# Sliding-window attention into a gated MLP: value loads requested nine steps later, and one transpose split by head halves

## The chip, the cores and the metric

The kernel runs on one core of a Trainium2 chip. The metric is the device time of one execution in microseconds (us), here the median of several runs of the same program. A profile of one execution shows what each engine did: PE (matrix multiply) and PEld (its weight loads), DVE (vector), ACT (activation), POOL (GpSimd), and SP, which only issues DMAs in this kernel.

## The reference

Attention with an ALiBi bias and a window of 128 keys over 8 batches of 8 heads, 576 tokens, head size 64; its output, as rows of 512, goes through two matrix products with a gate between them.

```python
scores = scale * np.matmul(q, k.transpose(0, 1, 3, 2))
bias = slopes[:, None, None] * (-np.abs(rel).astype(np.float32))[None, :, :]
mask = (rel >= 0) & (rel < window)
scores = np.where(mask, scores + bias[None], -1000000000.0)
attn = np.exp(scores - max) / sum          # softmax over the keys
x = np.matmul(attn, v)                     # heads side by side: [4608, 512]
h = x @ w_in                               # [4608, 2048]
g = h * (1.0 / (1.0 + np.exp(-beta * h)))
out = g @ w_out                            # [4608, 512], float32
```

## The kernel before, in words

**Tiling.** A batch has five blocks of queries and keys, four of 128 rows and one of 64 (ROWS). `load_qk` (L123) requests q and k of one block on SP's queue (L95, float32 into the staging tiles `fst`, 13 buffers) and returns a cast that POOL does later into `bst` (L129, 8 buffers, bf16). `TD` (L250, L253) transposes a cast block into `qkT` with two DMA transposes, q first, also on SP's queue; `qkT` has two copies, by batch parity. Batches 0 to 2 are transposed on PE instead (`TP`, L229, copied by L234, and `TT`). `load_v` (L134) fetches the values of one block: for batches 3 to 7 (NTE = 3) POOL issues a DMA that casts on its way (L137) straight into `vs`, which has two copies by batch parity; for batches 0 to 2 SP loads them and POOL casts (L142).

`SC` (L262) makes scores: matmuls of keys with queries into PSUM (L290) and the exponential on ACT (L303, or L298 for batches 0 and 1), then a mask on DVE (L307). `PV` (L319) multiplies the weights with the values (L330 and L334; a column of ones gives the sum), four heads at a time (g = 0 or 1), and DVE divides by the sum (L339, L340) into `xn`. `X` (L346) transposes the 512 columns of a finished block of `xn` into `XT`: by four PE transposes (L358) into a PSUM tile of the two-buffer pool `psum_t` and one copy by ACT or DVE (L363), and for batches above 3 by a DMA transpose on SP (L354).

The second part works on groups of 512 tokens: `HS` (L368) makes one 128-wide piece of h (L377: four matmuls, over the four 128-row pieces c of `XT`), with a tanh on ACT (L382) and the gate on DVE (L383). `OS` (L387) sums four matmuls of the output (L393); its sixteenth is scaled by ACT (L408) and stored by POOL (L411).

**Order.** The order of PE's instructions is written out by hand, and from batch 2 on that of SP and POOL too. The start of batch 0 is a straight list (from L589): scores, then for each block the second four heads of PV and the transpose of the block before, and then the first H group. From L651 on, `steps` lists the attention work; `merge` (L493) lays loads, casts and DMA transposes between the steps, each at a due step number counted from `first[b]`, the step at which batch b's scores begin (L507 to L511). A batch takes 21 to 23 steps. `spread` (L434) then interleaves these with the H and output pieces in proportion to costs; the laid-in loads cost zero.

The lines that the change touches:

```python
t0 = first[b] - 26 + 4.3 * sb                          # q and k of block sb requested
jobs.append((t0 + 4.5, lambda c=casts: c.pop()()))     # cast on POOL
jobs.append((t0 + 8.5, lambda b=b, sb=sb: TD(b, sb)))  # transposes on SP
vals(b, sb, first[b] - 16 + 3 * sb)                    # values requested on POOL
```

## Time and profile before

| what | value |
|---|---|
| median of 6 runs | 330.33 us (329.11 to 331.66) |
| the profiled execution's own time | 330.55 us |
| its span, first to last instruction | 328.6 us |
| PE, PEld busy | 314.9, 155.1 us |
| DVE, ACT, POOL busy | 193.6, 213.3, 107.3 us |
| SP's DMA queue (q1), POOL's (q0) | 105744 packets, 31.60 MB; 30224 packets, 15.54 MB |
| values by POOL (L137) | 25 requests, median 5.8 us from issue to landing for the 128-row ones |
| q and k loads by SP (L95, L109) | medians 5.0 and 5.8 us |

A line of the profile names a source line, an engine, what is written and read, and a count. In the timeline the first two numbers are the start and the length in microseconds; a bracket at the end is idle time of the engine before the instruction and what ended it. In the table by stretches a line gives the stretch, its length, busy time and instruction count of PE, PEld, DVE, ACT and POOL, the granted PE clock, the mean busy share of the 16 DMA engines (above 1 where packets of several queues overlap) and GB/s. In the list of waits a line gives who waited for whom, the total, the number of waits and the longest. The chain that ended last is followed backwards from the last instruction, at each step to what released it; "SPq" in it is SP's queue issuing, "DMA" the way from issue to landing.

### The profile page before, as it was taken

Reading aid. Unit: us, or ns where it says so; the run is one execution under the profiler, and the core shown is the slowest. Engines: PE = TensorE matmul, PEld = TensorE weight load, DVE = VectorE, ACT = ScalarE, POOL = GpSimd, SP = SyncE. Lnnn points to the kernel's source line nnn. Section 1 sums busy time; section 2 is a strip of 40 time slices with the busy share of each in tenths; the row PEclk is TensorE's granted clock in tenths of the full one; section 3 lists DMA queues with packets and bytes.
Section 4 is the critical chain, followed back from the end, with each engine's and each line's share of the span. In section 5 each row is a group of like instructions: output and inputs, shape, how many; then the busy total and the mean of one; then the engine's idle time right before and its main releaser. Section 6 shows DMA issues by size and latency. Waiting matters only on the chain.

```text
span 328.6 us, 6187 instructions
## 1 busy us (share of the span) xinstructions
PE 314.9 (96%) x2258; PEld 155.1 (47%) x2300; DVE 193.6 (59%) x421; ACT 213.3 (65%) x413; POOL 107.3 (33%) x173
## 2 busy tenths in 40 slices
PE   8978999999999999999999999999999999999995
PEld 3454445444544555454445444444445444444442
DVE  6657768995436777666666666666665443344400
ACT  5657685887787777777777777777774444454421
POOL 3754584155633545342443243500000000010000
PEclk9999999999999999999999999999999999999999
DMA  7999999999999999999999999934122200001011
GB/s 184 244 181 296 177 273 210 206 205 166 196 219 165 186 187 211 222 154 183 152 208 144 208 171 175 157 74 51 40 66 66 72 32 32 34 32 60 36 66 64
DMA packets 136174, 47.67 MB, mean 145 GB/s; under 512 B 123200, under 2 KB 133712, under 8 KB 136144
## 3 DMA queue, kind: packets, MB, share of 16 engines
q1 hardware_dynamic: 105744, 31.60, 54.1%
q0 software_dynamic: 30224, 15.54, 29.7%
q8 instruction: 18, 0.29, 0.4%
q10 hardware_dynamic: 176, 0.14, 0.1%
q14 instruction: 12, 0.10, 0.1%
HBM read 36.71 MB, written 9.44 MB: 140 GB/s over the span
## 4 chain that ended last, share of the span: by engine, by line
PE 68%; DMA 18%; SPq 8%; POOL 2%; issue 1%; DVE 0%; ACT 0%; POOLq 0%
PE ops L393 33%; PE hps L377 28%; DMA fst<-in_k_dram 8%; DMA fst<-in_v_dram 6%; DMA fst<-in_q_dram 4%; SPq L253 3%; SPq L109 3%; PE sps L290 3%; SPq L95 2%; PE pv L334 2%; PE pv L330 1%; DMA qkT<-bst 1%; POOL vs L142 1%; POOL bst L129 1%; POOL W L193 0%
## 5 line engine op out<-in xcount | busy, mean ns | idle before, releaser
L382 ACT ACTIVATE sig<-hps,beta_h 128x512 bf16<-128x512 f32 x144 | 99.8, 695 | 78.5 <-PE hps L377 61.3
L377 PE MATMUL hps<-XT,W 128*128 128x512 bf16 x554 | 144.2, 379 | 2.0 <-ACT XT L363 0.7
L393 PE MATMUL ops<-W,gT 128*128 128x512 bf16 x560 | 143.7, 379 | 1.4 <-issue 0.3
L383 DVE SCALAR_TENSOR_TENSOR gT<-sig,hps 128x512 bf16<-128x512 bf16 x144 | 98.3, 684 | 63.8 <-ACT sig L382 63.5
L393 PEld LDWEIGHTS <-gT 128*128 128x128 bf16 x576 | 53.5, 98 | 62.7 <-issue 2.1
L377 PEld LDWEIGHTS <-W 128*128 128x128 bf16 x576 | 51.5, 97 | 52.9 <-issue 3.0
L303 ACT ACTIVATE pt<-sps,bias 128x256 bf16<-128x256 f32 (+1 forms) x192 | 72.8, 492 | 2.1 <-PE sps L290 2.1
L129 POOL CAST bst<-fst 128x512 bf16<-128x512 f32 (+1 forms) x50 | 32.3, 648 | 78.9 <-DMA fst<-in_q_dram 45.9
L307 DVE TENSOR_TENSOR pt<-pt,mask 128x1024 bf16<-128x1024 bf16 x48 | 34.6, 720 | 34.7 <-ACT pt L303 34.5
L411 POOL DMA_DIRECT2D out_dram<-osb x32 | 17.9, 560 | 90.3 <-ACT osb L408 90.3
L340 DVE TENSOR_TENSOR xn<-pv,zs 128x256 bf16<-128x256 f32 (+1 forms) x80 | 33.7, 422 | 2.6
L408 ACT ACTIVATE osb<-ops 128x512 f32<-128x512 f32 x35 | 20.9, 597 | 15.2 <-PE ops L393 15.2
L334 PE MATMUL pv<-vs,pt 128*128 128x65 bf16 x320 | 28.7, 193 | 1.0 <-POOL vs L142 0.6
L334 PEld LDWEIGHTS <-pt 128*128 128x128 bf16 x320 | 21.6, 97 | 10.3 <-issue 0.6
L330 PE MATMUL pv<-vs,pt 128*128 128x65 bf16 x256 | 24.1, 193 | 0.3 <-DVE XT L363 0.3
L330 PEld LDWEIGHTS <-pt 128*128 128x128 bf16 x256 | 20.1, 98 | 7.5 <-issue 1.0
L290 PE MATMUL sps<-qkT 64*128 64x256 bf16 (+2 forms) x320 | 21.9, 251 | 1.8 <-DVE qkT L234 0.8
L298 ACT ACTIVATE pt<-sps 128x1024 bf16<-128x1024 f32 x16 | 16.3, 1023 | 8.8 <-PE sps L290 8.3
L137 POOL DMA_DIRECT2D vs<-in_v_dram x25 | 21.3, 853 | 0.6 <-issue 0.5
L290 PEld LDWEIGHTS <-qkT 64*128 64x128 bf16 x320 | 11.2, 94 | 20.1 <-issue 14.0
L339 DVE RECIPROCAL zs<-pv 128x4 f32<-128x4 f32 (+1 forms) x80 | 14.0, 176 | 10.4 <-PE pv L334 10.1
L113 POOL CAST bst<-fst 128x512 bf16<-128x512 f32 x24 | 14.5, 621 | 14.5 <-DMA fst<-in_q_dram 11.4
(49 smaller groups left out, 112.6 us busy)
## 6 DMA issues: line engine op xcount, KB each, us to landing
fst<-in_q_dram SPq DMA_DIRECT2D x32, 256.0 KB, 5.0
fst<-in_k_dram SPq DMA_DIRECT2D x32, 256.0 KB, 5.8
out_dram<-osb POOLq DMA_DIRECT2D x32, 256.0 KB, 3.4
fst<-in_v_dram SPq DMA_DIRECT2D x12, 256.0 KB, 6.5
vs<-in_v_dram POOLq DMA_DIRECT2D x20, 128.0 KB, 5.8
W<-in_moe_w_in_dram POOLq DMA_DIRECT2D x4, 512.0 KB, 7.9
W<-in_moe_w_out_dram POOLq DMA_DIRECT2D x4, 512.0 KB, 14.0
fst<-in_q_dram SPq DMA_DIRECT2D x8, 128.0 KB, 4.1
```

The costliest lines, as they stand in the source:

```text
L129: nc.gpsimd.tensor_copy(out=t[0 : ROWS[sb], i], in_=f)
L137: nc.gpsimd.dma_start(out=to, in_=v[b, :, P * sb : P * sb + ROWS[sb], :].rearrange("h p d -> p h d"))
L290: nc.tensor.matmul(o, lhsT=qk[64 * e : 64 * e + 64, 1, p, P * kb : P * kb + P], rhs=qk[64 * e : 64 * e + 64, 0, p, P * kb : P * kb + nq], ...
L303: nc.scalar.activation(out=pt[:, e, cols], in_=sps[e][:, cols], func=ACTF.Exp, scale=qscale, bias=bias[:, half, h : h + 1],)
L307: nc.vector.tensor_tensor(out=pt[:], in0=pt[:], in1=masks[m][:].rearrange("p (o c) -> p o c", o=1).broadcast_to([P, 2, 512]), op=ALU.mult,)
L330: nc.tensor.matmul(pv[:, hl, 0 : D + 1], lhsT=weights(b, qb - 1, h, 1), rhs=vs[:, qb - 1, h, 0 : D + 1], start=True, stop=False,)
L334: nc.tensor.matmul(pv[:, hl, 0 : D + 1], lhsT=weights(b, qb, h, 0), rhs=vs[:, qb, h, 0 : D + 1], start=qb == 0, stop=True,)
L340: nc.vector.tensor_tensor(out=xn[0:nq, 4 * g : 4 * g + 4, :], in0=pv[0:nq, :, 0:D], in1=zs[0:nq].broadcast_to([nq, 4, D]), op=ALU.mult,)
L377: nc.tensor.matmul(hps[:], lhsT=W1[:, c, bass.ts(j, P)], rhs=XT[:, c, c0 : c0 + TOKG], start=(c == 0), stop=(c == NDM - 1),)
L382: nc.scalar.activation(out=sig[:], in_=hps[:], func=ACTF.Tanh, scale=beta_h[:, j : j + 1])
L383: nc.vector.scalar_tensor_tensor(out=gts[g][:, j, :], in0=sig[:], scalar=1.0, in1=hps[:], op0=ALU.add, op1=ALU.mult)
L393: nc.tensor.matmul(ops_[:], lhsT=gT[:, j, i * P : i * P + P], rhs=W2[:, j, :], start=(j == 0), stop=(j == NFF - 1),)
```

## The change

**Values.** For batches 3 to 7 the request of block sb's values moves from step `first[b] - 16 + 3 * sb` to `first[b] - 7 + 3 * sb`. The due steps of q, k, casts and transposes stay.

**Head halves.** `X` takes an optional half. With half 0 it transposes the first two 128-column pieces (heads 0 to 3) and copies these; with half 1 the other two. Each call takes a PSUM tile of its own from `psum_t`. For block 3 of batch 0, the last block that the first H group reads, half 0 now stands before that block's second PV, and half 1 where the whole transpose stood.

```diff
-    def X(b, qb):
+    def X(b, qb, half=None):
         nq = ROWS[qb]
-        xnv = xns.pop((b, qb))[:].rearrange("p h d -> p (h d)")
+        cs = range(NDM) if half is None else range(2 * half, 2 * half + 2)
+        xnv = (xns[b, qb] if half == 0 else xns.pop((b, qb)))[:].rearrange("p h d -> p (h d)")
...
         xt = psum_t.tile([P, NDM, P], BF16, name="xt", tag="t")
-        for c in range(NDM):
+        for c in cs:
             nc.tensor.transpose(
                 out=xt[:, c, :], in_=xnv[:, c * P : (c + 1) * P], identity=ident[:]
             )
         copy = nc.vector.tensor_copy if b in (1, NTE) or (b, qb) == (0, 2) else nc.scalar.copy
+        c = slice(cs[0], cs[-1] + 1)
         for at, r0, r1 in parts:
-            copy(out=XT[:, :, at : at + r1 - r0], in_=xt[:, :, r0:r1])
+            copy(out=XT[:, c, at : at + r1 - r0], in_=xt[:, c, r0:r1])
...
-                vals(b, sb, first[b] - 16 + 3 * sb)
+                vals(b, sb, first[b] - 7 + 3 * sb)
...
                 if qb:
                     X(0, qb - 1)
-            X(0, NQB - 2)
+                if qb == 2:
+                    X(0, 3, 0)
+            X(0, 3, 1)
```

## The prediction

> **What bounds the kernel now.** I read the page first: busy shares, then the chain that ended last.

> ```profile
> PE 314.9 (96%) x2258; PEld 155.1 (47%) x2300; DVE 193.6 (59%) x421; ACT 213.3 (65%) x413; POOL 107.3 (33%) x173
> ...
> PE 68%; DMA 18%; SPq 8%; POOL 2%; issue 1%; DVE 0%; ACT 0%; POOLq 0%
> ```

> TensorE is busy for 96% of the span, so the most that any reordering can return is its idle time, 328.6 - 314.9 = 13.7 us. Yet a quarter of the chain is DMA and SP's queue. The table by stretches says where:

> ```profile
> 74.00:84.00 10.00, 9.68 (x88) 5.07 (x89) 4.31 (x11) 7.22 (x19) 5.01 (x8) 1.00 1.51 171
> 84.00:99.00 15.00, 13.99 (x118) 7.01 (x118) 7.52 (x17) 11.03 (x27) 8.42 (x13) 1.00 1.29 207
> 99.00:125.00 26.00, 25.79 (x198) 13.21 (x198) 17.51 (x38) 19.39 (x42) 11.16 (x17) 1.00 1.33 176
> 125.00:310.00 185.00, 183.69 (x1203) 88.97 (x1225) 106.23 (x212) 121.47 (x238) 43.48 (x68) 1.00 0.68 112
> ```

> The first two numbers of a line are its length and PE's busy time. From 99 us to 310 us PE idles 1.5 of 211 us, in pieces of some 0.05 us: nothing is to be had there. Up to 99 us a chain of loads and transposes decides. I followed it in order of time, and then looked at PE's own waits:

> ```profile
> 79.55 2.52 SPq L253
> ...
> 83.43 3.58 DMA fst<-in_q_dram
> ...
> 90.57 2.22 SPq L95
> ...
> 92.90 2.55 SPq L253
> ...
> 95.55 3.02 DMA qkT<-bst
> 98.56 0.05 issue
> 98.61 0.39 PE sps L290 x5
> ```

> ```profile
> PE sps L290 <- DMA qkT<-bst: 0.6, 1, 0.6
> PE hps L377 <- ACT XT L363: 0.7, 1, 0.7
> ```

> The chain enters PE at 98.6 us: the scores of batch 3's second half (L290) wait 0.56 us for the last DMA transpose of its keys. The other line is the wait ahead of the first H group, at 23.15 us. These are the two places that the two edits touch.

> [...] the queues' packets cover more than the engines' time (DMA share 1.51) while value loads run, and the first transpose of a pair then holds SP's queue for 2.12 and 2.52 us (74.46 and 79.55 us) instead of 1.2 to 1.3 us (70.04 and 71.90 us, before the first such load). [...] The trace has a median of 5.4 us (2.8 to 7.4) for these[...]

> **Part 1: values nine steps later.** Nothing is added or removed: 25 requests of L137, 0.89 us of POOL each, stand further back in POOL's queue. PE's and SP's orders stay as they were in the built program, apart from part 2's transposes. Batch 3's requests are now at:

> ```profile
> 74.59 1.76 POOL L137 DMA_DIRECT2D vs<-in_v_dram  x2
> ...
> 78.77 0.88 POOL L137 DMA_DIRECT2D vs<-in_v_dram  x1
> ...
> 85.21 0.88 POOL L137 DMA_DIRECT2D vs<-in_v_dram  x1
> ...
> 89.09 0.70 POOL L137 DMA_DIRECT2D vs<-in_v_dram  x1
> ```

> In the changed order the first stands behind the casts of block 3's q and k (84.53 + 0.73 in this trace), the second and third around those of block 4, the fourth behind those of batch 4's block 0 (about 91.5 us), and the short fifth behind those of its block 1 (98.5 us). So from 74 to 84 us three requests go away; from 84 us to the stall there are four instead of one and a half.

> What that is worth at 98.6 us: in the first stretch the two transposes overran 1.2 us by 0.9 and 1.3 us, 2.2 us for three requests, or 0.73 us a request. SP runs almost without a pause there, so this comes off the chain. In the second stretch 2.5 more requests at the same price put back 1.8 us. Net: the last transpose lands 2.2 - 1.8 = 0.4 us sooner, and PE's 0.56 us wait shrinks to 0.16 us. The price per request is my choice: it assumes that overrun grows with the number of requests. If the second stretch absorbs them (its overruns of 1.2, 1.6 and 1.35 us came with only one and a half, and three stores of outputs), the gain is the whole wait, 0.56 us; more can't be had, since PE then runs without a gap. From above, I take it that the three overruns of this stretch, 4.15 us together, double: less the 2.2 us saved, the transpose is 2 us late, a loss of 2 us.

> What is late next: batch 3's first scores start at 85.79 us and their last transpose of q landed at 85.5 us; that margin of 0.3 us grows, as its requests lie in the relieved stretch. Batch 4's first scores (115.05 us, transpose of q landed 113.9 us, margin 1.15 us) gain too: the two value loads at 98.5 us move behind them, leaving one short one. Its second half (131.8 us) has 7 us of margin (124.8 us), more than all the overrun above, and batches 5 to 7 have 8 to 12 us. The values themselves: batch 3's block 0 would land at about 85.3 + 0.9 + 5.4 = 92 us, and the first product with it is at 101.65 us, 10 us of cover; batch 4's, requested near 113 us, is used at 136.9 us. On POOL, what is queued behind a request is the next cast or store; those now come sooner by 0.89 us per request moved back, and the casts mostly wait for their own loads anyway (45.9 us of waits on q).

> **Part 2: the last output by head halves.** Added: one ACT copy, and one more use of a two-buffer PSUM pool. The 512-wide copy takes 0.585 us (22.52 us), and 128x256 ones 0.37 us (27.87, 97.27 us). Step by step: half 0's transposes need the buffer of the first output, free at 21.15 us; they start at 21.20 instead of nothing being there, so PV of block 3's second heads starts at 21.32, not 21.05 us (+0.27). Its normalization on DVE ends at 22.40, not 22.14 us. The DVE copy of output 2 follows, 22.42 to 22.84 us. Half 1 is transposed from 22.45 us and copied by ACT from 22.77 to 23.14 us. In the built program the H group's first matmul now waits for DVE alone and its third for ACT. It can start at 22.84 + 0.05 = 22.89 instead of 23.15 us, and the third at 22.89 + 2 x 0.215 = 23.32 us finds half 1 there. Gain at this place: 0.26 us; from below, if the buffer wait costs twice as much, nothing.

> But it doesn't reach the end:

> ```profile
> 29.59 0.40 PE L229 MATMUL tps<-ident,bst 128*128 128x128 bf16 x4 [0.39 <-POOL bst L113]
> ```

> ```profile
> 28.92 0.61 POOL L113 CAST bst<-fst 128x512 bf16<-128x512 f32 x1 [6.36 <-DMA fst<-in_q_dram]
> ```

> PE waits there for a cast of batch 1's q, and POOL for that load, issued at 21.04 us behind a value of batch 0 and not behind PE. PE would arrive 0.26 us sooner and wait 0.65 us. I cost part 2 at nothing; without that cover 0.26 us.

> **The sum.** Profiled execution: 330.55 us, a span of 328.6 us and 1.95 us around it. 328.6 - 0.40 - 0 = 328.2 us, or 330.15 us. The median of the six runs is 330.33 us, 0.2 us lower; from it 330.33 - 0.40 = 329.9 us.

> **Rivals.** (A) The forecast, the wait at 98.6 us mostly or wholly gone: 329.8 to 330.0 us. (B) Traffic only changes places: the last transpose lands when it did, or the gain of 0.4 us is used up by another wait of the same chain; 330.3 us. For it: the sum of bytes before 98 us is nearly the same. Against: the fifth request leaves that stretch and the first stretch's overruns are on the chain. (C) Slower: the four requests between 84 and 98 us hold up the transposes of blocks 3 and 4 on SP's queue, whose landing is already the last event before PE goes on. Every microsecond that it comes after 98.56 us is lost one for one, as nothing later is idle. At the 2 us bound: 332.3 us. For it: overruns are already largest there. Against: SP enters the stretch up to 2.2 us earlier. (D) Both edits pay: 0.56 + 0.26 us and half of PE's other 1.3 us of idle time between 62 and 98 us, 1.5 us in all: 328.8 us. Against: those waits name DVE, not DMA. That part 1 doesn't do what it says is settled by the built order; that part 2's group starts no earlier is covered in (A), at no cost.

> **How the numbers follow.** Chances: A 0.50, B 0.25, C 0.17, D 0.08. Prediction 329.9 us. The range takes A and B with the spread of the runs shown (329.11 to 331.66, so about 0.5 us for a median), reaches most of D and half of C: 328.9 to 331.9 us. A bound of 0.5%, 1.65 us, is about what a measurement of this kernel can tell from no change. Slower beyond it needs most of C: 0.15. Faster needs D and the spread on its side: 0.09. Within: 0.76.

> **What would show it.** Right: the transposes near 74.5 and 79.5 us hold SP's queue for about 1.2 us; PE's wait on qkT near 98.6 us is under 0.3 us; the H group starts near 22.9 us, and the wait near 29.6 us grows to about 0.65 us. Wrong: a wait on qkT above 0.6 us there or a new one near 115 us (C), a PE wait on a value load (no margin seen for that), or the first group's gain still present at 62 us.

## The result, and the profile after

The changed kernel takes 332.71 us (median of 37 runs, 329.92 to 336.13), the kernel before 330.21 us (median of 74 runs made beside it). The ratio is 1.006 with a 95% interval of 1.0046 to 1.0074, from which executions more than 1.5% above the fastest of their kernel are left out. So the change makes the kernel about 0.6% slower: rival (C), not the forecast. The profiled execution took 331.31 us, with a span of 329.3 us.

The table by stretches of the changed kernel, same columns as before:

```profile
74.00:84.00 10.00, 9.68 (x88) 5.07 (x89) 4.59 (x12) 7.22 (x18) 3.98 (x7) 1.00 0.88 170
84.00:99.00 15.00, 12.98 (x106) 6.53 (x106) 6.95 (x16) 10.42 (x25) 8.58 (x13) 1.00 1.62 202
99.00:125.00 26.00, 25.48 (x200) 13.21 (x204) 16.58 (x37) 18.70 (x40) 11.97 (x17) 1.00 1.52 185
125.00:310.00 185.00, 183.64 (x1202) 88.91 (x1225) 107.11 (x213) 121.64 (x240) 44.02 (x67) 1.00 0.68 111
```

The DMA share (second number from the end) fell from 1.51 to 0.88 in the first stretch and rose from 1.29 to 1.62 in the second: the traffic moved as the built order said. PE's busy time in the second stretch fell from 13.99 to 12.98 us, and nowhere else by as much as 0.4 us. PE's waits of the changed kernel, and its timeline there:

```profile
PE sps L290 <- DMA qkT<-bst: 2.1, 1, 2.1
```

```profile
96.95 0.28 PE L290 MATMUL sps<-qkT 64*128 64x256 bf16 x2
99.36 0.51 PE L290 MATMUL sps<-qkT 64*128 64x64 bf16 x10 [2.13 <-DMA qkT<-bst]
```

The wait for the last transpose of batch 3's keys is 2.13 us instead of 0.56 us. It grew at both ends: PE comes 0.8 us sooner (96.95 us; 97.76 us before) and the transpose lands 0.76 us later. Only the later landing costs time; it is the whole 0.7 us by which this execution's span is longer. The chain shows how it came late:

```profile
91.71 3.10 SPq L253
...
94.91 4.41 DMA qkT<-bst
99.32 0.05 issue
99.36 0.51 PE sps L290 x10
```

SP issued that transpose at 94.91 us, 0.64 us sooner than the 95.55 us of before, but it took 4.41 us to land instead of 3.02 us. The earlier issue isn't a gain of the change's own: SP was already 0.7 us ahead at the first transposes of batch 3 (69.33 us; 70.04 us before), before any of its values was requested in either kernel. SP's queue over the same time, in the changed kernel and then, for the last transposes, in the kernel before:

```profile
78.58 2.88 SPq L253 DMA_TRANSPOSE qkT<-bst  x2
...
84.25 5.04 SPq L253 DMA_TRANSPOSE qkT<-bst  x2
89.33 1.14 SPq L95 DMA_DIRECT2D fst<-in_q_dram  x1
90.53 0.61 SPq L95 DMA_DIRECT2D fst<-in_k_dram  x1
91.24 7.53 SPq L253 DMA_TRANSPOSE qkT<-bst  x4
```

```profile
86.17 3.71 SPq L253 DMA_TRANSPOSE qkT<-bst  x2
...
92.90 6.52 SPq L253 DMA_TRANSPOSE qkT<-bst  x4
```

The pair at 78.58 us is 1 us shorter than the 3.83 us of before, but the pair at 84.25 us (block 3) is 1.3 us longer, and the four from 91.24 us on (block 4, then the first block of batch 4) are 1.0 us longer.

The profile doesn't account for the whole loss. Its span is 0.7 us longer than before; the medians differ by 2.5 us. A part of what is missing shows in the granted PE clock, as a mean over each execution: 24 of the 38 executions had 0.995 or less, with a median of 333.3 us; the other 14 had a median of 331.1 us. The profiled one had 1.00.

### The profile page after: what moved, and what is told of

It reads as the page before. It is cut to its first block, busy times and chain, and to the rows that moved or that the text cites. A ratio compares the mean times of both kernels' runs of the same rounds, so it can differ in the third digit from the quotient of the medians.

```text
span 329.3 us, 6187 instructions
## 1 busy us (share of the span) xinstructions
PE 314.7 (96%) x2258; PEld 155.3 (47%) x2300; DVE 194.1 (59%) x421; ACT 213.2 (65%) x414; POOL 108.2 (33%) x173
## 4 chain that ended last, share of the span: by engine, by line
PE 81%; DMA 7%; SPq 4%; DVE 4%; issue 1%; ACT 1%; POOL 1%
PE hps L379 35%; PE ops L395 35%; PE sps L290 4%; PE pv L334 3%; DMA fst<-in_k_dram 2%; DMA fst<-in_q_dram 2%; PE pv L330 2%; SPq L253 2%; DMA fst<-in_v_dram 2%; DMA qkT<-bst 1%; DVE gT L385 1%; SPq L95 1%; SPq L109 1%; PE xt L359 1%; DVE qkT L234 1%
## 5 line engine op out<-in xcount | busy, mean ns | idle before, releaser
L385 DVE SCALAR_TENSOR_TENSOR gT<-sig,hps 128x512 bf16<-128x512 bf16 x144 | 98.2, 683 | 63.7 <-ACT sig L384 63.4
L129 POOL CAST bst<-fst 128x512 bf16<-128x512 f32 (+1 forms) x50 | 33.3, 669 | 81.8 <-DMA fst<-in_q_dram 46.7
L290 PE MATMUL sps<-qkT 64*128 64x256 bf16 (+2 forms) x320 | 21.9, 251 | 3.2 <-DMA qkT<-bst 2.1
L137 POOL DMA_DIRECT2D vs<-in_v_dram x25 | 21.4, 856 | 0.6 <-PE hps L379 0.5
L290 PEld LDWEIGHTS <-qkT 64*128 64x128 bf16 x320 | 11.2, 94 | 21.5 <-issue 14.0
L113 POOL CAST bst<-fst 128x512 bf16<-128x512 f32 x24 | 14.5, 619 | 15.2 <-DMA fst<-in_q_dram 10.2
```

What stands on the lines that cost most here:

```text
L129: nc.gpsimd.tensor_copy(out=t[0 : ROWS[sb], i], in_=f)
L137: nc.gpsimd.dma_start(out=to, in_=v[b, :, P * sb : P * sb + ROWS[sb], :].rearrange("h p d -> p h d"))
L290: nc.tensor.matmul(o, lhsT=qk[64 * e : 64 * e + 64, 1, p, P * kb : P * kb + P], rhs=qk[64 * e : 64 * e + 64, 0, p, P * kb : P * kb + nq], ...
L385: nc.vector.scalar_tensor_tensor(out=gts[g][:, j, :], in0=sig[:], scalar=1.0, in1=hps[:], op0=ALU.add, op1=ALU.mult)
```

## The experiments

All ratios are against the kernel before on the same chip. "Lowered" counts the executions with a mean granted clock of 0.995 or less; a mean of 0.998 is not counted, since in the four profiles that have it the clock drops only in the last 1.1 to 1.5 us, behind PE's last products. "Lands" is the last transpose of batch 3's keys in the profile, "wait" PE's wait for it; "issue" is how long the first transposes of batch 3's blocks 3 and 4 held SP's queue.

| kernel | median us | ratio (interval) | lowered | lands | wait | issue |
|---|---|---|---|---|---|---|
| before (first profile) | 330.21 | | | 98.56 | 0.56 | 2.41, 2.55 |
| both edits (first profile) | 332.71 | 1.006 (1.0046, 1.0074) | 24 of 38 | 99.32 | 2.13 | 3.73, 3.56 |
| values only | 332.60 | 1.0052 (1.0031, 1.0074) | 3 of 10 | 98.73 | 1.19 | 3.48, 3.46 |
| values only, again | 332.33 | 1.0069 (1.0045, 1.0094) | 5 of 10 | 100.16 | 2.68 | 4.33, 2.77 |
| halves only | 330.11 | 0.9994 (0.9972, 1.0016) | 0 of 14 | 99.42 | 1.42 | 2.80, 2.76 |
| before, again | 330.23 | 1.0004 (0.9984, 1.0023) | 2 of 14 | 98.64 | 0.98 | 2.55, 2.64 |
| both edits, again | 333.22 | 1.0081 (1.0049, 1.0112) | 3 of 6 | 100.66 | 3.47 | 3.26, 3.72 |
| batch 3's values only late | 331.36 | 1.0029 (1.0005, 1.0052) | 7 of 20 | 99.47 | 2.43 | 3.45, 2.98 |
| batches 4 to 7's only late | 330.39 | 1.0019 (0.9997, 1.0041) | 1 of 12 | 98.16 | 1.40 | 2.99, 2.63 |
| no values of batch 3 | 329.58 | 0.9967 (0.9949, 0.9985) | 0 of 20 | 95.99 | none | 2.43, 1.84 |
| halves, transposes first | 329.62 | 0.9973 (0.9953, 0.9993) | 0 of 20 | 94.65 | none | 1.25, 2.99 |
| both edits, wait filled | 331.64 | 1.0033 (1.0015, 1.0051) | 0 of 22 | 100.27 | 0.72 | 3.77, 3.46 |
| both edits, transposes first | 329.69 | 0.9969 (0.9953, 0.9986) | 0 of 22 | 97.02 | none | 1.25, 3.03 |
| before, transposes first | 329.40 | 0.9970 (0.9952, 0.9987) | 0 of 22 | 97.31 | none | 1.25, 2.84 |

**Which edit: each alone, and both kernels again.** The values' new steps alone:

```diff
-                vals(b, sb, first[b] - 16 + 3 * sb)
+                vals(b, sb, first[b] - 7 + 3 * sb)
```

> The values' new due steps alone; block 3 of batch 0 is transposed whole, as before. Theory (traffic): the four value loads that now lie between the casts of batch 3's last blocks and 98 us hold up the last transposes of its keys. PE's wait on qkT near 98.6 us is 1 to 2 us instead of 0.56 us and the time is 1.5 to 2.5 us above before, nearly the whole loss. Rival (halves): the head halves are at fault; then this equals before within 0.5 us. Second part of the theory (clock): where the wait is long, PE's granted clock drops in that execution, so runs at a granted clock below 1.0 are some 2 us slower than runs at 1.0, and more of them are below 1.0 than with the kernel before.

The halves alone are the changed kernel with `first[b] - 16` put back.

> The head halves alone; the values keep their due steps. Theory: the first H group starts 0.3 to 0.4 us sooner against the start of block 3's work, and PE's wait near 98.6 us grows from 0.56 us by what PE is ahead, so the time equals before within 0.5 us, and the granted clock is as before. Rival (halves at fault): 1.5 us or more above before. A third view, that this is a pure gain that the values then hid: 0.3 to 0.8 us below before.

> The kernel before, unchanged, for a second profile of it and for the granted clock of each execution. All views: ratio 1.0. Theory (clock): its wait of some 0.6 us is too short to lower the clock, so nearly all executions show 0.998 or 1.0, and a rare one at 0.995 is about 2 us slower. Rival to the clock: the same shares at 0.995 as in the changed kernel, so that the clock is a matter of the chip and not of the wait.

> The changed kernel, unchanged, for a second profile and more clocks. All views: 1.5 to 2.5 us above before. Theory (clock): more than half of the executions below 1.0, the wait near 97 us at 2 us or more in the profile; if this profile falls in an execution with a lowered clock, the lowered stretch begins with the wait near 97 us[...]. Rival: the lowered stretch lies at the start or end.

The values alone carry the loss (332.60 us), the halves alone equal before (330.11 us). The wait in these two profiles doesn't tell them apart, though, 1.19 against 1.42 us: it differs from execution to execution, and one profile of each isn't enough. The second profile of both edits fell on an execution with a lowered clock. PE's timeline of it, and the same instructions in the kernel before:

```profile
96.95 0.28 PE L290 MATMUL sps<-qkT 64*128 64x256 bf16 x2
100.71 0.82 PE L290 MATMUL sps<-qkT 64*128 64x64 bf16 x10 [3.47 <-DMA qkT<-bst]
101.46 1.89 PE L395 MATMUL ops<-W,gT 128*128 128x512 bf16 x4
103.15 1.91 PE L379 MATMUL hps<-XT,W 128*128 128x512 bf16 x4
104.85 1.59 PE L395 MATMUL ops<-W,gT 128*128 128x512 bf16 x4
106.28 0.29 PE L334 MATMUL pv<-vs,pt 128*128 128x65 bf16 x4
106.41 1.02 PE L379 MATMUL hps<-XT,W 128*128 128x512 bf16 x4
```

```profile
98.61 0.51 PE L290 MATMUL sps<-qkT 64*128 64x64 bf16 x10 [0.56 <-DMA qkT<-bst]
99.05 1.04 PE L393 MATMUL ops<-W,gT 128*128 128x512 bf16 x4
...
101.65 0.29 PE L334 MATMUL pv<-vs,pt 128*128 128x65 bf16 x4
```

and the table by stretches of the same execution, in which the value after POOL's is the granted clock:

```profile
90.00:97.00 7.00, 6.95 (x52) 3.35 (x51) 2.82 (x6) 5.80 (x14) 3.60 (x6) 1.00 2.15 185
...
99.20:106.00 6.80, 5.29 (x21) 2.15 (x22) 1.57 (x3) 3.71 (x9) 2.11 (x5) 0.50 1.19 219
106.00:112.00 6.00, 5.95 (x44) 2.90 (x44) 3.23 (x8) 2.92 (x5) 2.50 (x5) 1.00 1.35 187
```

At 99.15 us, while PE waits, its clock is halved, and it stays so until 105.97 us. Four matmuls take 1.89 us instead of 1.04 us. Aligned with the kernel before, PE is 2.1 us late when the scores start and 4.6 us late at 106 us: 2.5 us more for a wait that had already cost its own length.

The clock was lowered for 6.83 us here and for 3.41 us in the profile of "batch 3's values only late", and these stretches began 92.16 and 95.57 us after the clock had been raised at the start. In the first profiles of both kernels it fell 324.27 us after it had been raised, behind PE's last products. These five times are 2, 1, 27, 28 and 95 times 3.413 us; such steps of 3.413 us, counted from where the clock was raised, are called windows from here on. The lines below show windows around the wait in four executions (the clocks were raised at 6.99, 4.55, 6.25 and 6.80 us): both edits again and batch 3's values only late, with one window each, then both edits (first profile) and the values only (again), with two. The first numbers of a line are the window, its length and PE's busy time; the third from the end is the clock.

```profile
95.73:99.15 3.42, 1.51 (x11) 0.61 (x9) 1.44 (x3) 1.61 (x4) 0.99 (x2) 1.00 1.59 227
```

```profile
96.71:100.13 3.42, 0.99 (x14) 0.53 (x14) 0.69 (x1) 0.97 (x2) 2.85 (x5) 1.00 1.30 223
```

```profile
94.99:98.40 3.41, 2.24 (x15) 0.92 (x13) 2.08 (x5) 2.23 (x4) 1.91 (x4) 1.00 1.53 243
98.40:101.82 3.42, 2.46 (x20) 1.29 (x21) 0.60 (x2) 2.13 (x6) 0.54 (x1) 1.00 1.12 193
```

```profile
95.55:98.96 3.41, 1.97 (x14) 0.81 (x11) 1.88 (x5) 2.08 (x4) 1.11 (x2) 1.00 1.52 235
98.96:102.38 3.42, 2.17 (x18) 1.12 (x19) 0.24 (x1) 1.85 (x5) 1.33 (x3) 1.00 1.15 172
```

In the first two PE idles 1.91 and 2.43 us of one window, and the next window runs at half the clock. In the last two the waits of 2.13 and 2.68 us are cut by a window's end, into 1.17 and 0.96 us and into 1.44 and 1.24 us, and the clock stays. So in these four the place of the wait on the windows decides, and not its length alone: behind a wait of 2.43 us the clock fell, and behind one of 2.68 us it didn't. All 14 profiles fit this: every window at full clock with 1.91 us or more of idle PE was followed by the halved clock (16 windows, all but two of them at the end of the program), none with 1.54 us or less was (about 1300). The limit between the two is worked out from these traces; no run was made to test it.

Two things keep the clock from being the whole loss. One window at half the clock costs at most 1.7 us, an estimate: half of its 3.41 us. By their mean clock, 0.995 over a span of some 330 us, 21 of the 24 lowered executions had one window, yet the 24 are 2.2 us slower than the other 14: the rest must come from something else, perhaps from longer waits in these executions, which was not shown. And with the values alone the 12 executions that were not lowered have a median of 332.3 us, still 1.9 us above the kernels before beside them (330.4 us). So the lateness itself is a large part of the loss; the experiment that fills the wait, below, gives its size.

The kernel before is nearly free of the lowered clock: over the runs beside four groups of these experiments, 8 of 168 executions were lowered.

**Which batches.** In `vals(...)`, the old offset for all but batch 3, or for batch 3 alone:

```diff
-                vals(b, sb, first[b] - 7 + 3 * sb)
+                vals(b, sb, first[b] - (7 if b == NTE else 16) + 3 * sb)
```

> The changed kernel, but the values of batches 4 to 7 keep the old due steps: only batch 3's are later. Theory (traffic beside the last transposes of batch 3): all of the loss is here, 1.5 to 2.5 us above before, PE's wait near 97 us 1.2 to 3.5 us, and part of the executions at a granted clock of 0.995 or lower. Rival (later batches, whose values now meet the next batch's q and k): equal to before within 0.5 us.

> The changed kernel, but batch 3's values keep the old due steps: batches 4 to 7 alone are later. Theory: equal to before and to the halves alone within 0.5 us, wait near 98 us 0.6 to 1.5 us, no wait on a DMA after 100 us, granted clock 0.998 to 1.0 nearly always. Rival: 1.5 us or more above before.

Batch 3's values alone give 1.0029, 7 of 20 lowered, and a wait of 2.43 us; the later batches' alone give 1.0019 with an interval that includes 1, one of 12 lowered. The direction is the theory's, the size less than it said (1.0 us instead of 1.5 to 2.5 us). The intervals overlap, so a part from batches 4 to 7 isn't excluded.

**Is it the traffic of these loads.** Batch 3's value loads are left out (the products then use what batch 1 left in the buffer):

```diff
+                if b > NTE:
-                vals(b, sb, first[b] - 7 + 3 * sb)
+                    vals(b, sb, first[b] - 7 + 3 * sb)
```

> The changed kernel with batch 3's five value loads left out, so batch 3 is computed with the values that batch 1 left in the buffer. Theory (these loads' traffic slows SP's queue): the last transpose of batch 3 lands 2 us or more before PE needs it or at least with under 0.3 us of wait, first transposes of blocks 3 and 4 hold SP's queue 1.2 to 2 us instead of 3.6 us, clock at 1.0, time 0.3 to 0.9 us below before. Rival (SP's queue is slow there for its own loads and the stores, whatever the values do): the transposes still hold it for 2.5 us or more and the wait stays above 0.8 us.

The transpose lands at 95.99 us, 3.3 us sooner than with the change, no wait is left, and no execution is lowered. SP's queue in this kernel:

```profile
74.52 3.46 SPq L253 DMA_TRANSPOSE qkT<-bst  x2
...
79.34 2.73 SPq L253 DMA_TRANSPOSE qkT<-bst  x2
...
85.03 4.90 SPq L253 DMA_TRANSPOSE qkT<-bst  x2
...
91.30 5.83 SPq L253 DMA_TRANSPOSE qkT<-bst  x4
```

Two things are to be seen. With no value load at all, the pair at 74.52 us still takes 3.46 us, as in the other kernels: that overrun doesn't come from the values, nor from any other transfer that POOL issued, as none is in flight there. And of the 7.5 us that the four transposes from 91 us on held the queue, 1.7 us go. These loads are the cause of the late landing; a part of each overrun is not theirs. For the later pairs that part isn't settled: POOL's stores of outputs, issued at 83.01, 88.01 and 91.04 us, run beside SP's own loads there.

**Or does the order on SP's queue decide.** The values keep their old steps; batch 3's transposes are due 0.6 of a step sooner, so those of blocks 3 and 4 stand ahead of the next q and k loads instead of behind them:

```diff
-                jobs.append((t0 + 8.5, lambda b=b, sb=sb: TD(b, sb)))
+                jobs.append((t0 + (7.9 if b == NTE else 8.5), lambda b=b, sb=sb: TD(b, sb)))
```

> Head halves, values at the old due steps, and batch 3's transposes due 0.6 of a step sooner, which puts those of blocks 3 and 4 ahead of the next q and k loads on SP's queue instead of behind them. Theory (SP's queue order and what is in flight in it decide when the last transpose lands): it lands 1.5 to 3 us sooner, the wait near 97.5 us is gone, clock at 1.0, time 0.5 to 1.2 us below before. Rival (the transposes then wait for their casts with the loads behind them): the wait stays, or another opens near 115 us for batch 4, time equal to before or up to 1 us above.

The last transpose lands at 94.65 us, and the scores follow without a gap:

```profile
95.28 1.03 PE L379 MATMUL hps<-XT,W 128*128 128x512 bf16 x4
96.24 0.62 PE L290 MATMUL sps<-qkT 64*128 64x256 bf16 x12
96.79 1.04 PE L395 MATMUL ops<-W,gT 128*128 128x512 bf16 x4
```

The first transpose of block 3 now holds the queue for 1.25 us instead of 2.80 us, with one pair of q and k loads just ahead of it instead of two. The kernel is faster than before, 0.9973 (0.9953 to 0.9993).

**Is the lowered clock from the idling.** The whole change, with eight matmuls of zeros ahead of the scores that wait:

```diff
-            SC(b, m, p)
+            SC(b, m, p, fill=8 if (b, m, p) == (NTE, 1, 0) else 0)
```

> The changed kernel with eight matmuls of zeros (1.7 us at full clock) into the score tile ahead of batch 3's second-half scores, so that PE works through most of the wait near 97 us instead of idling. Theory (clock): the last transpose lands as late as in the changed kernel, but PE no longer idles for over 2 us, so hardly any execution shows a granted clock of 0.995 or lower, and the time is that of the changed kernel's executions at 1.0, 331.0 us, 0.7 to 1.2 us above before. Rival (the lowered clock is not from the idling): the same share of executions at 0.995 and the same 2 to 2.5 us above before, or more by what the matmuls add.

```profile
97.50 1.89 PE L218 MATMUL sps<-zero 128*128 128x512 bf16 x8
...
100.32 0.51 PE L290 MATMUL sps<-qkT 64*128 64x64 bf16 x10 [0.72 <-DMA qkT<-bst]
```

None of 22 executions is lowered, against 27 of 44 with the change (both groups) and 6 of 59 of the kernel before on the same chip, though the transpose lands as late as ever, at 100.27 us. So here the idling is what lowers the clock. The ratio falls from 1.006 to 1.0033, some 0.9 us by useless work in the gap; the two intervals just overlap, so the size isn't firm. What is left, 1.35 us in medians, goes with the lateness itself, by this the larger part of the loss.

**What the edits are worth without the wait.** The transposes first, with the whole change and with the kernel before:

> The whole change, and batch 3's transposes due 0.6 of a step sooner, ahead of the next q and k loads on SP's queue. Theory: what hurts is that the last transpose lands after PE gets there; with it sooner by 3 us or so the later values cost nothing: no wait near 97 us, clock at 1.0, time 0.5 to 1.2 us below before, equal to the same without the later values. Rival (the values' traffic still delays it): a wait of 0.3 to 1 us stays and the time is between.

> The kernel before, with batch 3's transposes due 0.6 of a step sooner and nothing else. Tells what the head halves are worth once no DMA wait stands behind them. Theory (the halves' 0.3 to 0.4 us reach the end when the wait near 98 us is gone): 0.3 to 0.6 us below before, so 0.3 to 0.4 us slower than with the halves. The prediction's view (the halves are swallowed by the wait near 29.6 us): the same as with the halves, 0.6 to 1.0 us below before.

329.69 us with both edits, 329.62 us with the halves, 329.40 us with neither: within their spread the three are equal. The values' new steps do no harm that shows once the transpose lands in time, and no gain of either edit shows. In the profile of the last kernel another wait of 1.41 us, for batch 4's transposes, opens at 115.86 us; in the other two it doesn't. A gain of 0.3 us by the halves can't be seen in medians of this spread.

**The share of lowered executions, once more.**

> The values' new due steps alone once more, for the share of executions at a lowered clock, of which ten were too few. Theory A (the halves matter here: they bring PE to the wait some 0.4 us sooner, so it is longer and lowers the clock more often): the share at 0.995 or lower is a third or less, against 27 of 44 with both edits, and the median lies 1.0 to 1.8 us above before. Theory B (the values alone do it all): a share of a half or more and 2 to 2.5 us above before.

5 of 10, and 8 of 20 together with the first time, against 27 of 44 with both edits. Neither theory's share is met by the two groups together; the medians (2.0 us above before in each group) are close to theory B's: the values alone make the loss. Whether the halves raise the share of lowered executions, by bringing PE to the wait sooner, stays open at these numbers.

## Why the prediction was wrong, point by point

**What bounds the kernel: right.** One place decides, the last transpose of batch 3's keys, and almost nothing after it is idle. All kernels in which it lands in time are at 329.4 to 329.7 us.

**Part 1, the price of a request: the step that failed.** "0.73 us a request" took the two overruns of the first stretch, 0.9 and 1.3 us, as the value loads' doing. That loads on POOL's queue hold up transposes on SP's was the author's assumption; the run without batch 3's value loads shows how far it holds, with the last transpose landing at 95.99 instead of 99.32 us. After the change the two overruns are 0.95 us (2.15 us held, 1.2 us without overrun) and 0.36 us: 0.93 us is saved, not 2.2 us, and the first stays without any value load. The lines on which the price rests could have raised the doubt: that transpose starts at 74.46 us, before POOL's first request at 74.59 us. In the second stretch the two first transposes grew by 1.32 and 1.01 us, 2.3 us, against 1.8 us forecast; a k load that held the queue 1.6 us too long before doesn't do so now. So far the issues about balance, and SP's lead of 0.7 us is kept. What the sum left out altogether is the way from the issue to the landing: 4.41 instead of 3.02 us, 1.4 us. The landing was forecast 0.4 us sooner and came 0.76 us later in the first profile. Over the profiles with batch 3's values late and no other edit near them it is at 98.7 to 100.7 us (five profiles, mean 99.7 us), with them at the old steps at 98.2 to 99.4 us (four, mean 98.7 us).

**"Every microsecond that it comes after 98.56 us is lost one for one": the second failure.** It was said in rival (C), and its bound of 332.3 us rests on it. Waits that left 1.91 and 2.43 us of one window idle were followed by a halved clock for 6.83 and 3.41 us, which would add 3.4 and 1.7 us if PE worked all the while (an estimate, half of each); 2.5 us were measured in the first, where PE still idled at the start. The prediction treated idle time as costing its own length, and no view of the kernel before could show otherwise, its waits being short.

**Part 2: the size nearly right, the place of its cover wrong, the sum right.** From the wait for batch 0's values to the H group, PE needs 4.03 us instead of 4.39 us: 0.36 us gained, 0.26 us forecast. PV of block 3's second heads starts at 21.73 us, as worked out (21.32 us) if the 0.41 us by which this profile is later there is added, and the group starts 0.05 us after DVE's copy ends (23.15, 23.20 us), as worked out too. The wait of 0.17 us for a buffer at 22.30 us, ahead of the transposes of output 2, was not foreseen. The gain was to be swallowed near 29.6 us, with a wait there of 0.65 us. PE doesn't wait there in the profile after:

```profile
29.16 0.40 PE L229 MATMUL tps<-ident,bst 128*128 128x128 bf16 x4
```

The second profile of the kernel before has no wait there either: the 0.39 us belonged to one execution. The halves alone still equal before; in their profile the wait on the last transpose is 1.42 us. It is consistent with the gain ending in that wait, but the waits of single profiles differ too much to show it.

**What is late next: right.** Batch 4's first scores start at 115.80 us without a wait, and no product waits for a value load after 20 us.

**The chances.** Rival (C) had 0.17 and the range ended at 331.9 us; the 0.15 put on a time slower than that leaves almost none of (C) inside the range, which was said to hold half of it. The three overruns were known to be largest in the stretch that received the loads; that was named as evidence for (C) and then outweighed by a saving read from two durations of one execution.

## What to carry to other kernels

The DMA requests that were moved away from some transfers here were moved onto others, and the last transpose took 4.41 us to land instead of 3.02 us: look first which transfer ends the next wait of the bounding engine, and count its time from issue to landing as well as what holds its queue. Here the order on the queue was the better lever: transposes ahead of loads that nobody needs yet gave 0.3% (0.9970) and made both edits indifferent. A wait on PE was dearer than its length where the clock halved behind it: one of 3.47 us cost 2.5 us more, while one of 2.68 us, cut by a window's end, left the clock at 1.00. Useless matmuls in the wait took the ratio from 1.006 to 1.0033, in intervals that just overlap.
